# Second MLP's weight conversion in another order, its tiles in other homes, and the reciprocal kept in PSUM

## The chip, the core and the metric

The kernel runs on one core of a Trainium2 chip. Its engines work side by side, each through its own instructions in order: TensorE (PE, matrix products), VectorE (DVE), ScalarE (ACT), GpSimd (POOL); SyncE (SP) issues most of the transfers. The metric is the device time of one execution in microseconds (us), lower is better. Three runs of the kernel before took 1035.93 to 1036.97 us, median 1036.37.

## What is computed

Attention over 4 batches, 8 heads, 576 positions and 64 elements gives x with 2304 rows (tokens) of 512. Two MLPs follow, each with an inner width of 2048; the second one's middle is a rational function:

```python
def _moe_ref(x, w_in, w_out):                  # first MLP
    h = x @ w_in
    g = np.maximum(h, 0.0) + np.log1p(np.exp(-np.abs(h)))
    return g @ w_out

def _moe2_ref(x, w_in, w_out, a, b):           # second MLP
    h = x @ w_in
    P = a[0] + a[1] * h + a[2] * h * h + a[3] * h * h * h
    Q = 1.0 + np.abs(b[0]) * np.abs(h) + np.abs(b[1]) * h * h
    return (P / (Q + 1e-06)) @ w_out
```

Inputs come as float64. A product of nearly full precision is made of three products of rounded parts: each operand is a high part plus a low part (`hi`, `lo`), and hi·hi, hi·lo and lo·hi are summed.

## The kernel before

**Units.** An MLP is worked through in units (phase, T, ff): phase 0 or 1 is the first or second MLP, T a tile of 256 to 512 tokens, ff one of 16 slices of 128 of the inner width. `stage_a` makes h of the unit in a PSUM bank, `stage1` to `stage3` make the middle function and its two parts, `stage_b` adds the unit's share of the second product, three units after `stage_a`. Phase 0 has T 0 to 5; attention is interleaved until T 4 begins. Phase 1, T 0 follows unit by unit (16 units of 384 tokens). T 1 to 3 of phase 1 run in another way: `group` makes four blocks of 256x512 by seven sums of products (`slot`), where combinations of weights (areas `s1` to `s4`) and of tokens take the place of an eighth product; there are four groups to a T. T 4 (`TAIL`) is again 16 units of 384 tokens.

**The second MLP's weights.** 32 blocks (ff, half), half 0 of the first product and half 1 of the second, are loaded raw (512 KB each) and converted while phase 0, T 4 and 5 run (`conv2_to`, one to a unit). `conv_t` (L909 and L911 on DVE, L910 on ACT) makes a float32 tile of tag `tc`; `conv_hl` splits it into hi (ACT L915) and lo (POOL L916). Of each pair of half-0 blocks `sum_make` forms the combinations (DVE, L980 to L983, four instructions), and `sum_split` splits and stores these in the DRAM areas `wa_d` (ACT L991, POOL L992, one store, twice to a pair). The order in the list `c2`: half 1 of ff 0 to 11, both halves of ff 12 to 15, then half 0 of ff 0 to 11.

**Homes.** Half 1 of ff 0 to 11 lies in SBUF areas that attention has left (tags J, Q, V). Half 0 of ff 0 to 11 lies in tag W, where the first MLP's `w1h` of the same number must have been used for the last time. Both halves of ff 12 to 15 are spilled to DRAM (`w2_d`, 16 stores) and reloaded during phase 1, T 0 (`reload2`, 16 loads), half 1 into W. `keep_a` stores half 0 of all 16 into `wa_d` (32 stores), from which T 1 to 4 load 100 tiles `wa` of 512 KB into W, 11 slots ahead (`load_wa`; 7 of them by the end of T 0).

**The quotient.** In phase 1, 1/Q is made as exp(-ln Q) on ACT and corrected on DVE; with `w` = Q, `a` = the reciprocal, `t` = the numerator without its constant:

```python
        nc.scalar.activation(a, w, AF.Ln, bias=qc)                                           # stage2: L1212
        nc.scalar.activation(a, a, AF.Exp, scale=-1.0)                                       # L1213
        nc.vector.scalar_tensor_tensor(w, w, c, a, op0=ALU.add, op1=ALU.mult)                # L1214
        nc.vector.scalar_tensor_tensor(w, w, -2.0, a, op0=ALU.add, op1=ALU.mult)             # L1215
        nc.vector.scalar_tensor_tensor(t, t, nega[:, 0:1], w, op0=ALU.add, op1=ALU.mult)     # L1216
```

Units use this `stage2`, with all operands in SBUF. The groups' blocks use `act2` (L1243 to L1247), which is the same but for the reciprocal, written into h's own bank; the correction L1246 goes to `w` in SBUF. `stage1` reads h last at L1203 (numerator; the groups' L1237).

**Banks.** PSUM has eight banks: four `acc`, two `h`, two `at`. Units of phase 1, T 0 use only the two `h` up to ff 4 and alternate between `h` and `at` from ff 5 on (`hsel`), as do those of T 4. In a group three sums lie in `h` banks (called y, v and w in the code) and one in `at`.

**The order.** Each tile pool hands out buffers in program order. `plan` then simulates the program with a table of costs, orders each engine's instructions by how late each may end, and ties them in that order for all that starts before 936 us of its own time; the rest keeps the program's priorities.

Of the kernel before, what the change touches and what calls it, by code (L numbers as in the profile page):

```python
# [338 lines left out]
def moe_chain_kernel(ctx, tc, qk0, v0, qk, vv, s0, s, w1, w2, ab, out):  # L339
# [658 lines left out]
    def home2(ff, half):  # L998
        if half == 0:
            if ff >= FS:  # L1000
                return t_l("w2h", [128, 512], F32R), t_l("w2l", [128, 512], F32R)
# [9 lines left out]
    def reload2(ff):
        for half in range(2):
            w2_t[ff, half] = home2(ff, half)
            for d, t in zip(w2_d[ff, half], w2_t[ff, half]):
                nc.sync.dma_start(out=f(t), in_=d)
# [190 lines left out]
    def stage2(u):  # L1206
# [466 lines left out]
```

## Time and profile before

| | |
|---|---|
| median of three runs | 1036.37 us |
| the profiled execution | 1037.39 us, its span 1035.6 us |
| PE busy | 1002.6 us (97%) |
| weight loads (beside PE) | 902.5 us (87%) |
| DVE busy | 814.8 us (79%) |
| ACT busy | 803.7 us (78%) |
| POOL busy | 477.5 us (46%) |
| mean granted clock of TensorE | 0.998 |
| moved by DMA | 207.92 MB |

Stages in the span: attention and phase 0 up to T 3 until about 465 us; phase 0, T 4 and 5, from there to 617; phase 1, T 0, from 617 to 697; the groups of T 1 to 3 from 695 to 957; T 4 to the end. A time in the rows counts from the start of the span. An idle time in brackets is that before the instruction, and behind the arrow stands what ended it.

### The profile page before, as it was taken

What the parts mean: (1) busy time and instruction counts of PE and PEld (TensorE: products, weight loads), DVE (VectorE), ACT (ScalarE), POOL (GpSimd) and SP (SyncE); (2) the same over time, 40 slices, a digit from 0 to 9 for tenths busy, and PEclk for the clock granted to TensorE, in tenths of its full rate; (3) what the DMA queues carried; (4) which work ended last, traced back from release to release, by engine and by line L of the source; (5) the groups of instructions that cost most, each with busy time, mean ns of one, the idle gap of its engine ahead of it and who ended that gap; (6) DMA issues with size and microseconds to landing.
All of it is one profiled execution on the core that took longest, in us unless ns stands there. A gap on an engine that the chain in (4) does not pass through costs nothing.

```text
span 1035.6 us, 18274 instructions
## 1 busy us (share of the span) xinstructions
PE 1002.6 (97%) x5924; PEld 902.5 (87%) x5924; DVE 814.8 (79%) x1783; ACT 803.7 (78%) x1652; POOL 477.5 (46%) x464
## 2 busy tenths in 40 slices
PE   6999999999999999999999999998999999999998
PEld 5889999889998888898999888788888898889897
DVE  5788986887987788785455879898789888778865
ACT  5898878877987777777677676788878888787775
POOL 2757664412221121222226766776566457455543
PEclk9999999999999999999999999999999999999999
DMA  9777565665564644436679988969555655654300
GB/s 265 279 241 262 184 223 187 207 187 151 160 199 126 201 147 146 134 118 215 228 241 310 371 282 294 362 210 312 178 164 186 216 187 173 205 169 156 123 1 31
DMA packets 103502, 207.92 MB, mean 201 GB/s; under 512 B 11632, under 2 KB 28848, under 8 KB 103408
## 3 DMA queue, kind: packets, MB, share of 16 engines
q1 hardware_dynamic: 100864, 202.60, 59.3%
q10 hardware_dynamic: 2544, 4.16, 1.6%
q8 instruction: 47, 0.77, 0.3%
q14 instruction: 47, 0.39, 0.1%
HBM read 163.25 MB, written 39.39 MB: 196 GB/s over the span
## 4 chain that ended last, share of the span: by engine, by line
PE 62%; DVE 15%; ACT 9%; issue 5%; POOL 4%; DMA 4%; SPq 0%; DVEq 0%; POOLq 0%; ACTq 0%
PE at L764 5%; PE h L1089 5%; PE h L1090 5%; PE h L1091 5%; PE acc L1127 4%; PE acc L1125 4%; PE acc L1126 4%; PE at L1330 4%; PE h L1330 3%; PE acc L1270 3%; PE at L623 2%; PE acc L1269 2%; PE acc L1268 2%; PE at L624 2%; DVE tc L911 2%
## 5 line engine op out<-in xcount | busy, mean ns | idle before, releaser
L616 POOL TENSOR_SCALAR PA<-PA,stat 128x384 f32<-128x384 f32 (+3 forms) x112 | 72.1, 650 | 172.4 <-DVE stat L615 72.4
L1089 PE MATMUL h<-xs,w1h 128*128 128x448 f32 (+1 forms) x360 | 122.9, 342 | 1.9 <-DVE e L1191 1.9
L1090 PE MATMUL h<-xs,w1h 128*128 128x448 f32 (+1 forms) x360 | 122.5, 340 | 0.0
L1091 PE MATMUL h<-xs,w1l 128*128 128x448 f32 (+1 forms) x360 | 122.2, 340 | 0.0
L1126 PE MATMUL acc<-gl,w1h 128*128 128x448 f32 (+1 forms) x352 | 118.7, 339 | 1.2 <-POOL gl L1387 1.2
L1127 PE MATMUL acc<-gh,w1l 128*128 128x448 f32 (+1 forms) x352 | 119.0, 341 | 0.1
L1125 PE MATMUL acc<-gh,w1h 128*128 128x448 f32 (+1 forms) x352 | 118.6, 340 | 0.0
L1254 POOL TENSOR_TENSOR gl<-PA,gh 128x512 fp32r<-128x512 f32 x48 | 63.7, 1328 | 71.9 <-issue 54.9
L613 ACT ACTIVATE PA<-PA,stat 128x384 f32<-128x384 f32 (+3 forms) x112 | 64.0, 572 | 16.7 <-DVE stat L596 15.6
L1089 PEld LDWEIGHTS h<-xs,w1h 128*128 128x128 f32 x360 | 67.9, 189 | 6.5 <-DVE e L1191 3.1
L1090 PEld LDWEIGHTS h<-xs,w1h 128*128 128x128 f32 x360 | 67.8, 188 | 3.8 <-DVE xs L1054 0.4
L1091 PEld LDWEIGHTS h<-xs,w1l 128*128 128x128 f32 x360 | 67.8, 188 | 3.1
L1126 PEld LDWEIGHTS acc<-gl,w1h 128*128 128x128 f32 x352 | 66.1, 189 | 4.5 <-POOL gl L1387 1.4
L1127 PEld LDWEIGHTS acc<-gh,w1l 128*128 128x128 f32 x352 | 66.0, 188 | 3.8 <-DMA w1l<-l_d 0.3
L1125 PEld LDWEIGHTS acc<-gh,w1h 128*128 128x128 f32 x352 | 66.1, 189 | 3.0 <-ACT gh L1385 0.2
L1187 ACT ACTIVATE e<-h 128x448 f32<-128x448 f32 (+1 forms) x90 | 43.4, 482 | 30.6 <-PE h L1091 28.8
L1387 POOL TENSOR_TENSOR gl<-e,gh 128x256 fp32r<-128x256 f32 (+1 forms) x48 | 47.6, 992 | 33.8 <-ACT gh L1385 28.9
L1268 PE MATMUL acc<-w2b,gh 128*128 128x512 f32 x144 | 57.0, 396 | 0.5 <-ACT gh L1253 0.5
L1269 PE MATMUL acc<-w2b,gh 128*128 128x512 f32 x144 | 56.7, 394 | 0.0
L1270 PE MATMUL acc<-w2b,gl 128*128 128x512 f32 x144 | 55.1, 396 | 0.6 <-POOL gl L1254 0.6
L596 DVE CUSTOM_DVE_ANT_0 PA<-at,mask 128x384 f32<-128x384 f32 (+3 forms) x100 | 50.4, 518 | 5.8 <-PE at L624 4.2
L623 PE MATMUL at<-ht 128*128 128x512 f32 (+3 forms) x156 | 53.3, 347 | 0.6 <-DVE stat L604 0.3
(357 smaller groups left out, 3283.2 us busy)
## 6 DMA issues: line engine op xcount, KB each, us to landing
wa<-wa_d SPq DMA_DIRECT2D x100, 512.0 KB
w1l<-l_d SPq DMA_DIRECT2D x138, 256.0 KB
raw<-in_w_dram SPq DMA_DIRECT2D x48, 512.0 KB
raw<-in_qk_dram SPq DMA_DIRECT2D x24, 384.0 KB
l_d<-w1l SPq DMA_DIRECT2D x32, 256.0 KB
raw64x<-in_w_dram SPq DMA_DIRECT2D x16, 512.0 KB
wa_d<-pt SPq DMA_DIRECT2D x16, 512.0 KB
wa_d<-w2a SPq DMA_DIRECT2D x24, 256.0 KB
```

What stands on the lines that cost most here:

```text
L616: nc.gpsimd.tensor_scalar(pt[:, 0:n], pt[:, 0:n], stat[:, i, 2:3], 1.0, op0=ALU.mult, op1=ALU.mult)
L623: nc.tensor.matmul(o, hq, p.ht[:, 1, k0:k0 + n], start=True, stop=False)
L1089: nc.tensor.matmul(h, wh[:, cs], xh, start=(k == 0), stop=False)
L1090: nc.tensor.matmul(h, wh[:, cs], xl, start=False, stop=False)
L1091: nc.tensor.matmul(h, wl[:, cs], xh, start=False, stop=(k == KD - 1))
L1125: nc.tensor.matmul(o, wh[:, cs], gh, start=first and not both, stop=False)
L1126: nc.tensor.matmul(o, wh[:, cs], gl, start=False, stop=False)
L1127: nc.tensor.matmul(o, wl[:, cs], gh, start=False, stop=last and (not both or m % 2 == 1))
L1268: nc.tensor.matmul(acc[m], gh[:, cs], wh, start=first, stop=False)
L1269: nc.tensor.matmul(acc[m], gh[:, cs], wl, start=False, stop=False)
L1270: nc.tensor.matmul(acc[m], gl[:, cs], wh, start=False, stop=last)
L1330: nc.tensor.matmul(o[:, p * 256:p * 256 + 256], x, z[:, k], start=first and p == k == n == 0, stop=(k, n) == (1, 2), skip_group_check=True)
```

## The change

It does four things. Half-0 blocks are converted first, all 16 of them, then half 1; the 16 half-0 conversions are spread over 19 units, and the half-1 conversions follow, one to a unit, from the fifth unit of T 5 to the fourth of phase 1. Half 0 of ff 0 to 11 takes the homes that attention left, and half 1 of all 16 takes W. Only half 0 of ff 12 to 15 is spilled, straight into its place in `wa_d`, so that 8 stores to and 8 loads from there remain of 16 and 16, and 24 of the 32 stores at T 0. The tiles `wa` go through J, Q and V instead of W (12 places, as before) and are asked for from ff 6 on, 10 of them by the end of T 0. And `quotient` serves both kinds of units: in units from ff 5 on, in T 4 and in the groups the reciprocal and its corrected value both stay in h's bank.

```diff
 def conv2_hl(ff, half, t):
-        if ff >= FS:
+        spill = half == 0 and ff >= FS
+        if spill:
             hi, lo = (tmp_tile("PA", 3, (128, 512), F32R) for _ in range(2))
...
-        if ff >= FS:
-            for d, t in zip(w2_d[ff, half], (hi, lo)):
-                nc.sync.dma_start(out=d, in_=f(t))
+        if spill:
+            store_a(ff, (hi, lo))
...
     def home2(ff, half):
-        if half == 0:
-            if ff >= FS:
-                return t_l("w2h", [128, 512], F32R), t_l("w2l", [128, 512], F32R)
-            t = t_w("w2a", [128, 1024], F32R)
+        if half:
+            t = t_w("w2b", [128, 1024], F32R)
...
         else:
-            t = (t_q if ff < 10 else t_v if ff < FS else t_w)("w2b", [128, 1024], F32R)
+            t = (t_q if ff < 10 else t_v)("w2a", [128, 1024], F32R)
...
     def stage2(u):
...
-        nc.scalar.activation(a, w, AF.Ln, bias=qc)
-        nc.scalar.activation(a, a, AF.Exp, scale=-1.0)
-        nc.vector.scalar_tensor_tensor(w, w, c, a, op0=ALU.add, op1=ALU.mult)
-        nc.vector.scalar_tensor_tensor(w, w, -2.0, a, op0=ALU.add, op1=ALU.mult)
-        nc.vector.scalar_tensor_tensor(t, t, nega[:, 0:1], w, op0=ALU.add, op1=ALU.mult)
+        r, o = (h_t[u],) * 2 if T or ff >= H_ONLY else (a, w)
+        quotient(a, t, w, r, o)
...
+    def quotient(a, t, w, r, o):
+        nc.scalar.activation(a, w, AF.Ln, bias=qc)
+        nc.scalar.activation(r, a, AF.Exp, scale=-1.0)
+        nc.vector.scalar_tensor_tensor(w, w, QC, r, op0=ALU.add, op1=ALU.mult)
+        nc.vector.scalar_tensor_tensor(o, w, -2.0, r, op0=ALU.add, op1=ALU.mult)
+        nc.vector.scalar_tensor_tensor(t, t, nega[:, 0:1], o, op0=ALU.add, op1=ALU.mult)
...
     def act2(bl):
...
+        quotient(a, t, w, bl.h, bl.h)
...
-            t = t_w("wa", [128, 2, 2, 256], F32R)
+            t = home_a()
...
-        c2 = [(ff, 1) for ff in range(FS)] + [(ff, half) for ff in range(FS, NF) for half in range(2)] + [(ff, 0) for ff in range(FS)]
+        c2 = [(ff, half) for half in range(2) for ff in range(NF)]
...
-                if 0 < t4 <= 20:
-                    conv2_to(t4)
-                elif t4 > 20:
-                    conv2_to(min(t4, 32))
+                if t4 > 0:
+                    conv2_to(min(t4 * 16 // 19, 16) if t4 < 20 else min(t4 - 3, 32))
...
-                    keep_a(ff)
+                    if ff < FS:
+                        store_a(ff, w2_t[ff, 0])
...
-                    if ff >= 9:
-                        load_wa(min(ff - 8, 7))
+                    if ff >= 6:
+                        load_wa(min(ff - 5, 10))
```

Until about 450 us every engine's instructions stand as before. Three places after that, all on DVE. The first is phase 0, T 4, between the ends of two units' middle function (`at<-at,e`); `gl` is a unit's lo part, L909 and L911 convert. Before:

```order
L1191 SCALAR_TENSOR_TENSOR at<-at,e 128x448
L1387 TENSOR_TENSOR gl<-at,gh 128x448
L909 TENSOR_SCALAR tc<-raw64x 128x512
L911 SCALAR_TENSOR_TENSOR tc<-raw64x,tc 128x512
L1191 SCALAR_TENSOR_TENSOR h<-h,e 128x448
L1387 TENSOR_TENSOR gl<-h,gh 128x448
L909 TENSOR_SCALAR tc<-raw_7045 128x512
L911 SCALAR_TENSOR_TENSOR tc<-raw_7045,tc 128x512
```

Behind it, the same two units after the change, in whose numbering L907 and L909 convert and L978 to L981 form the sums:

```order
L1194 SCALAR_TENSOR_TENSOR at<-at,e 128x448
L1397 TENSOR_TENSOR gl<-at,gh 128x448
L907 TENSOR_SCALAR tc<-raw64x 128x512
L909 SCALAR_TENSOR_TENSOR tc<-raw64x,tc 128x512
L978 TENSOR_TENSOR tc<-tc 128x256
L979 TENSOR_TENSOR tc<-tc 128x256
L1194 SCALAR_TENSOR_TENSOR h<-h,e 128x448
L980 TENSOR_TENSOR tc<-tc 128x256
L1397 TENSOR_TENSOR gl<-h,gh 128x448
L981 TENSOR_TENSOR tc<-tc 128x256
L907 TENSOR_SCALAR tc<-raw_6849 128x512
L909 SCALAR_TENSOR_TENSOR tc<-raw_6849,tc 128x512
```

Four sums have come between; they stood in T 5 and at the start of phase 1. The second place is phase 1, T 0, from the numerator of its third unit (first row) to that of its fourth (last row). Before:

```order
L1203 SCALAR_TENSOR_TENSOR PA<-PA,prm,h 128x384
L911 SCALAR_TENSOR_TENSOR tc<-raw_7902,tc 128x512
L1163 COPY yb<-at 128x448
L1163 COPY yb<-acc 128x448
L909 TENSOR_SCALAR tc<-raw64x 128x512
L1214 SCALAR_TENSOR_TENSOR tmp<-tmp,e 128x384
L911 SCALAR_TENSOR_TENSOR tc<-raw64x,tc 128x512
L1215 SCALAR_TENSOR_TENSOR tmp<-tmp,e 128x384
L1216 SCALAR_TENSOR_TENSOR PA<-PA,prm,tmp 128x384
L1202 TENSOR_TENSOR PA<-PA,h 128x384
```

After, where L1221 to L1223 are the corrections and L1206 the numerator:

```order
L1206 SCALAR_TENSOR_TENSOR PA<-PA,prm,h 128x384
L1166 COPY yb<-at 128x448
L1221 SCALAR_TENSOR_TENSOR tc<-tc,e 128x384
L907 TENSOR_SCALAR tc<-raw_8026 128x512
L1222 SCALAR_TENSOR_TENSOR tc<-tc,e 128x384
L1221 SCALAR_TENSOR_TENSOR tmp<-tmp,e 128x384
L1223 SCALAR_TENSOR_TENSOR PA<-PA,prm,tc 128x384
L909 SCALAR_TENSOR_TENSOR tc<-raw_8026,tc 128x512
L1222 SCALAR_TENSOR_TENSOR tmp<-tmp,e 128x384
L1205 TENSOR_TENSOR PA<-PA,h 128x384
L1223 SCALAR_TENSOR_TENSOR PA<-PA,prm,tmp 128x384
L1206 SCALAR_TENSOR_TENSOR PA<-PA,prm,h 128x384
```

One conversion and one copy have left this stretch, and corrections of the unit ahead have come in. The third place is a group of T 2, where `h<-at,pt` puts a block into the `h` bank that the block just before it leaves (L1356 before, L1366 after). Before:

```order
L1245 SCALAR_TENSOR_TENSOR P_10092<-P_10092,h 128x512
L1246 SCALAR_TENSOR_TENSOR P_10092<-P_10092,h 128x512
L1356 TENSOR_TENSOR h<-at,pt 128x512
L1247 SCALAR_TENSOR_TENSOR PA<-PA,prm,P_10092 128x512
L1356 TENSOR_TENSOR h<-h,pt 128x512
```

After:

```order
L1221 SCALAR_TENSOR_TENSOR P_10036<-P_10036,h 128x512
L1222 SCALAR_TENSOR_TENSOR h<-P_10036,h 128x512
L1223 SCALAR_TENSOR_TENSOR PA<-PA,prm,h 128x512
L1366 TENSOR_TENSOR h<-at,pt 128x512
L1366 TENSOR_TENSOR h<-h,pt 128x512
```

The last correction now reads the bank and so stands ahead of the instruction that takes the bank over.

## Rows read from the trace of the kernel before

**Rows 1.** Windows by stage: length, busy us of PE, PEld, DVE, ACT, POOL; clock, DMA.

```profile
475.00:580.00 105.00, 105.00 (x518) 96.95 (x518) 61.12 (x92) 74.82 (x139) 42.48 (x33) 1.00 0.79 263
580.00:621.40 41.40, 39.60 (x195) 35.94 (x194) 31.13 (x38) 28.07 (x53) 27.66 (x21) 1.00 0.91 319
621.40:697.00 75.60, 71.22 (x348) 62.30 (x347) 67.03 (x96) 56.48 (x109) 53.01 (x42) 0.98 0.85 295
697.00:722.00 25.00, 22.40 (x147) 19.69 (x146) 21.79 (x29) 20.43 (x37) 17.17 (x14) 1.00 0.85 295
722.00:957.00 235.00, 233.27 (x1441) 207.69 (x1441) 193.37 (x272) 190.31 (x321) 136.48 (x103) 1.00 0.55 183
957.00:1035.60 78.60, 72.90 (x353) 63.32 (x351) 55.17 (x93) 55.25 (x104) 35.52 (x33) 1.00 0.16 51
```

**Rows 2.** Waits of PE, 590 to 725 us: us in total, times, longest.

```profile
PE acc L1132 <- ACT gh L1385: 2.3, 3, 1.4
PE h L1089 <- DVE PA L1203: 2.2, 1, 2.2
PE h L1089 <- DVE e L1191: 1.8, 2, 1.4
PE h L1330 <- issue: 1.2, 1, 1.2
```

**Rows 3.** Waits of PE, 957 to 1035 us.

```profile
PE acc L1132 <- DVE yb L1274: 1.4, 1, 1.4
```

**Rows 4.** Timeline of PE, phase 1, T 0: start, us, instruction, idle before.

```profile
645.83 0.44 PE L1089 MATMUL h<-yt,w2a 128*128 128x384 f32 x1 [2.23 <-DVE PA L1203]
```

**Rows 5.** A window just behind it; the clock stands behind the busy times.

```profile
646.30:649.70 3.40, 3.40 (x12) 3.05 (x11) 3.26 (x6) 2.72 (x6) 1.43 (x2) 0.50 1.03 319
```

**Rows 6.** Timeline of DVE in the same place.

```profile
638.72 1.40 DVE L1214 SCALAR_TENSOR_TENSOR tmp<-tmp,e 128x384 f32<-128x384 f32 x1 [0.49 <-ACT e L1213]
640.04 1.78 DVE L911 SCALAR_TENSOR_TENSOR tc<-raw64x,tc 128x512 int32<-128x512 int32 x1
643.14 1.51 DVE L1216 SCALAR_TENSOR_TENSOR PA<-PA,prm,tmp 128x384 f32<-128x384 f32 x1
```

**Rows 7.** Groups of DVE, 621.4 to 697 us: shapes, count, busy us, mean ns, idle.

```profile
L1203 DVE SCALAR_TENSOR_TENSOR PA<-PA,prm,h 128x384 f32<-128x384 f32 x10 | 6.1, 607 | 0.1
L1214 DVE SCALAR_TENSOR_TENSOR P<-P,e 128x384 f32<-128x384 f32 x4 | 4.4, 1094 | 0.7 <-ACT e L1213 0.7
L1216 DVE SCALAR_TENSOR_TENSOR PA<-PA,prm,P 128x384 f32<-128x384 f32 x4 | 2.4, 610 | 0.0
L911 DVE SCALAR_TENSOR_TENSOR tc<-raw64x,tc 128x512 int32<-128x512 int32 x2 | 3.4, 1686 | 0.1
L909 DVE TENSOR_SCALAR tc<-raw64x 128x512 int32<-128x512 int32 x2 | 1.6, 820 | 0.1
L983 DVE TENSOR_TENSOR tc<-tc 128x256 f32<-128x256 f32 x3 | 2.0, 652 | 0.1
```

**Rows 8.** Groups of DVE, 580 to 621.4 us.

```profile
L911 DVE SCALAR_TENSOR_TENSOR tc<-raw,tc 128x512 int32<-128x512 int32 x3 | 3.6, 1195 | 1.0 <-ACT raw L910 0.9
L980 DVE TENSOR_TENSOR tc<-tc 128x256 f32<-128x256 f32 x3 | 2.9, 977 | 0.3
```

**Rows 9.** Groups of DVE over the span, blocks of T 1 to 3.

```profile
L1246 DVE SCALAR_TENSOR_TENSOR tc<-tc,h 128x512 f32<-128x512 f32 x12 | 8.2, 686 | 0.4
L1247 DVE SCALAR_TENSOR_TENSOR PA<-PA,prm,tc 128x512 f32<-128x512 f32 x24 | 21.8, 909 | 0.4
```

**Rows 10.** Timeline where an `h` bank passes from one block to the next, twice.

```profile
720.02 0.69 DVE L1246 SCALAR_TENSOR_TENSOR tc<-tc,h 128x512 f32<-128x512 f32 x1
720.81 0.59 PE L1330 MATMUL h<-xl,wa 128*128 128x256 f32 x3 [1.17 <-issue]
...
806.85 0.69 DVE L1246 SCALAR_TENSOR_TENSOR tc<-tc,h 128x512 f32<-128x512 f32 x1
807.64 0.36 PE L1330 MATMUL h<-xl,wa 128*128 128x256 f32 x1
```

More of the change, by code (lines that the diff above doesn't have):

```diff
@@ L346, in moe_chain_kernel @@
     l_d = [[dr.tile([128, 512], F32, name=f"l_d{t}_{i}") for i in range(2)] for t in range(NF)]
-    w2_d = {(ff, half): [dr.tile([128, 512], F32, name=f"w2_d{ff}_{half}_{i}") for i in range(2)]
-            for ff in range(FS, NF) for half in range(2)}
     wa_d = [[dr.tile([128, 2, 1024], F32, name=f"wa_d{q}_{d}") for d in range(4)] for q in range(4)]
@@ L1007, in home2, with row_a, store_a @@
         else:
-            t = (t_q if ff < 10 else t_v if ff < FS else t_w)("w2b", [128, 1024], F32R)
+            t = (t_q if ff < 10 else t_v)("w2a", [128, 1024], F32R)
         return t[:, 0:512], t[:, 512:1024]
+    def row_a(ff):
+        q, p, i = ff // 4, ff // 2 % 2, ff % 2
+        return wa_d[q][i][:, p].rearrange("p (b h c) -> p b h c", b=2, h=2)
+    def store_a(ff, ts):
+        for h, t in enumerate(ts):
+            nc.sync.dma_start(out=row_a(ff)[:, :, h], in_=f(t).rearrange("p (b c) -> p b c", b=2))
     def reload2(ff):
[L1012 to L1015, printed above, removed]
+        w2_t[ff, 0] = t_l("w2h", [128, 512], F32R), t_l("w2l", [128, 512], F32R)
+        for h, t in enumerate(w2_t[ff, 0]):
+            nc.sync.dma_start(out=f(t).rearrange("p (b c) -> p b c", b=2), in_=row_a(ff)[:, :, h])
     def segments(T):
@@ L1210, in stage2 @@
         a, t, w = e_t[u]
-        c = QC
+        r, o = (h_t[u],) * 2 if T or ff >= H_ONLY else (a, w)
+        quotient(a, t, w, r, o)
+        e_t[u] = t
+    def quotient(a, t, w, r, o):
         nc.scalar.activation(a, w, AF.Ln, bias=qc)
-        nc.scalar.activation(a, a, AF.Exp, scale=-1.0)
-        nc.vector.scalar_tensor_tensor(w, w, c, a, op0=ALU.add, op1=ALU.mult)
-        nc.vector.scalar_tensor_tensor(w, w, -2.0, a, op0=ALU.add, op1=ALU.mult)
-        nc.vector.scalar_tensor_tensor(t, t, nega[:, 0:1], w, op0=ALU.add, op1=ALU.mult)
-        e_t[u] = t
+        nc.scalar.activation(r, a, AF.Exp, scale=-1.0)
+        nc.vector.scalar_tensor_tensor(w, w, QC, r, op0=ALU.add, op1=ALU.mult)
+        nc.vector.scalar_tensor_tensor(o, w, -2.0, r, op0=ALU.add, op1=ALU.mult)
+        nc.vector.scalar_tensor_tensor(t, t, nega[:, 0:1], o, op0=ALU.add, op1=ALU.mult)
     class Block:
@@ L1306, in moe_chain_kernel, with home_a @@
     wa_t, wa_n, used = {}, [0], [0]
+    wa_free = []
+    def home_a():
+        if not wa_free:
+            wa_free.extend([t_j] * 2 + [t_q] * 6 + [t_v] * 2)
+        al = wa_free.pop(0)
+        if al is not t_j:
+            return al("wa", [128, 2, 2, 256], F32R)
+        if "j" not in keep:
+            t = t_j("wa", [128, 2, 1024], F32R).rearrange("p n (b h c) -> p n b h c", b=2, h=2)
+            keep["j"] = t[:, 1]
+            wa_free.insert(0, t_j)
+            return t[:, 0]
+        return keep.pop("j")
     def load_wa(n):
@@ L1315, in load_wa @@
             wa_n[0] += 1
-    def keep_a(ff):
-        q, p, i = ff // 4, ff // 2 % 2, ff % 2
-        dst = wa_d[q][i][:, p].rearrange("p (b h c) -> p b h c", b=2, h=2)
-        for h, t in enumerate(w2_t[ff, 0]):
-            nc.sync.dma_start(out=dst[:, :, h], in_=f(t).rearrange("p (b c) -> p b c", b=2))
     def slot(T, q, a, b, o, first):
```

5 lines of the change are left out of this document (removed).

## The prediction, made before the changed kernel had run

> **What bounds the kernel now.** I read the windows by stage first [rows 1]. From 475 to 580 us PE has no idle time: its own work is the bound, and whatever DVE or the transfers do there is hidden. The idle time of PE that this change can reach is in four of the other windows: 41.40 - 39.60 = 1.8 us up to 621, 75.60 - 71.22 = 4.4 in the next (phase 1, T 0), 2.6 from 697 to 722, 1.7 in the 235 us of the groups. The last window has 5.7, of which one wait of 1.4 can move [rows 3]; most of the rest lies behind the last product. In the window of T 0, DVE is busy for 67.03 of 75.60 us (89%) and from 697 on for 87%: there it is DVE that PE waits for. The list of waits says the same [rows 2]: 2.2 us for a bank that L1203 on DVE still read, 1.8 for L1191 on DVE, 2.3 for a gh whose quotient DVE had just ended.
>
> The largest single wait is that of 2.23 us at 645.83 [rows 4]. Just ahead of it DVE worked on corrections and a conversion that took 1.40, 1.78 and 1.51 us [rows 6], though the same kinds of instruction take 0.61 elsewhere in the window (L1216 with `P` [rows 7]). POOL is busy for 53 of the 75.6 us [rows 1]; instructions of DVE whose tensors all lie in SBUF are drawn out there, and L1203, which reads h from PSUM, is not: 0.607 us over ten [rows 7]. Behind that wait the granted clock was 0.50 for 3.4 us [rows 5], the lower of the two levels, 1.2 GHz. What 12 products did in this time they would have done in half of it, so the wait of 2.23 us cost a further 1.7. Waits of 1.2 to 1.4 us [rows 2] left the clock of their windows at 1.00 [rows 1].
>
> **The change, part by part.** PE's instructions stay the same; so each part is worth what it does to these waits. Gains are negative.
>
> Sums move from T 5 and phase 1 into T 4 (475 to 580 us). The order puts four sums to two units there. By the slow rows of windows in which conversions and sums already run side by side, two units in T 4 would need on DVE: two middle functions and two lo parts that read PSUM, 4 x 0.61 as L1203 [rows 7], 2.4; two conversions of 0.82 (L909 [rows 7]) and 1.20 (L911 [rows 8]), 4.0; four sums of 0.98 (L980 [rows 8]), 3.9; together 10.3 us. PE did 518 products in 105 us there [rows 1], 0.203 each, 24 to a unit, so 9.8 for two units. With the sums at 0.65 (L983 [rows 7]) DVE's part is 9.0 us. In a window that has this mixture now PE lost 1.8 us (580 to 621 [rows 1]). Bounds: 0 and 0.5 us for each of 8 pairs, 4.0. With DVE at 61 of 105 us now [rows 1], I take **+0.8**.
>
> The store and load of half 1 of four slices goes, 24 transfers of 256 KB on SP's queue in all with the stores of `keep_a`; 8 MB of stores from the sums move into T 4, where the transfers' share is 0.79, from where it is 0.91 [rows 1]. As PE lost little at 0.91 and nothing that names a transfer [rows 2], this is 0 on both sides. Tiles `wa` are asked for earlier; PE did not wait for one [rows 2], 0.
>
> From 580 to 621 the sums thin out on DVE and their splits on POOL. The wait before the first unit of phase 1 (1.4 us, the longest of the two for L1191) stood behind such work. Half-1 conversions still stand there. Between 0 and -1.8 I take **-0.8**.
>
> Phase 1, T 0 (621 to 697). By the order, nine sums leave this stretch, 9 x 0.7 = 6.3 us between L983 and L980 [rows 7, 8], and three conversions come in, 3 x (1.4 + 0.6) = 6.0, L911 being 1.69 at most and L909 0.82 [rows 7]. Exchange for nothing, then. The quotient is what lightens it: of 16 units 11 (ff 5 to 15) keep the reciprocal and its correction in the bank, and the corrections of 9 of these lie in the stretch, 27 instructions. The 42 on L1214 to L1216 took 35.5 us, 0.85 each, between rows of 0.61 and 1.09; with one operand in PSUM I take L1203's 0.607 at most, 0.58 for the three: 27 x 0.27 = 7.3 us. DVE comes down from 67 to 60, below the 69.5 that PE needs (71.22 less the 1.7 of the slow clock). The gain is bounded by what PE lost there, 4.4 + 1.7 = 6.1. It won't all go: the first five units keep their corrections in SBUF, and they are where the long wait is. Between the numerators of units 3 and 4, DVE now has eight instructions ahead, as before: these took 9.1 us, the three longest in [rows 6], with two copies, two L911 and one L909 among them; after, six corrections at 0.85, one conversion and one copy, about 7.7. So the wait of 2.23 becomes 0.8, too short for the slow clock as far as these rows go: -1.4 - 1.7; half of the later waits, -0.9. **-4.0.**
>
> From 697 to 722 the wait of 1.4 us for gh ends behind two corrections of over 1.1 us. They go to 0.58: between 0 and -1.4, with the wait of the next paragraph 0.2 longer, **-1.0**.
>
> The groups (722 to 957). The correction L1247 takes 909 ns from SBUF [rows 9] and would take 690, as L1246 with its PSUM operand does; but PE lost only 1.7 us here, so at most that is gained. Against it: h's bank is now held through the last correction, 0.69 us longer, and the instruction that takes the bank over stands behind it on DVE, as the order shows. This bank is tight. PE's first product into it came 0.10 us after L1246 had ended, both at 720.81 and at 807.64 [rows 10]; the former wait, named "issue", ended with that release. Over eleven groups this gap is 0.1 to 1.5 us, 0.63 in the mean. Two blocks follow each other in that bank to a group, so up to 1.38 us are added to a turn. Less drawn-out work on DVE, about 1 us to a group, should give most of it back: between -1.7 and +8.3, I take **+0.7**.
>
> Here a rule speaks against the change. The rows show no price for an operand in PSUM: 0.607 on L1203 and 0.610 on L1216 from SBUF alone [rows 7]. The Trainium skill ("Perfetto Trace Analysis", Optimizing Scalar/DVE Operations) states an overhead of some 60 ns for an instruction of DVE on SBUF and 125 on PSUM. By that an estimate holds the bank 0.13 us longer to a block, 22 blocks, +2.9 on the sum. I go by the rows.
>
> The last units: the wait of 1.4 for a copy queued on DVE [rows 3] halves, **-0.5**.
>
> Sum: 0.8 - 0.8 - 4.0 - 1.0 + 0.7 - 0.5 = -4.8. The profiled execution took 1037.39 us, so 1032.6; it lies 1.0 above the median of the runs, so the prediction is **1031.6**.
>
> **Rivals.** *The bank becomes the bound (slower).* The turn from block to block in one `h` bank grows by 1.38 us to a group, 0.63 is free, and nothing is given back: 11 x 0.75 = 8.3 instead of 0.7. Sum +2.8, 1039.2. For it: the 0.10 us of [rows 10]. Against it: the planner knows the banks and may hurry those blocks, and DVE, at 193 of 235 us, has room. It decides from 0.5 us lost to a group on. *Given back elsewhere (no change).* T 4 costs its 4.0, as DVE there reaches the slow durations, or the early units of phase 1 stay as they are because conversions replaced the sums one for one: -1.5 for T 0 instead of -4.0, and 1.6 for T 4. Sum -1.6 or -1.5, 1034.9. For it: the even exchange above. *All the waits go.* 1.8 + 6.1 + 2.6 + 1.4 = 11.9, nothing given back: 1024.5. For it: DVE falls below PE in every window.
>
> **How the numbers follow.** 0.50 for the forecast, with 1028 to 1034.5 as its own range, 0.17 for all the waits, 0.17 for no change, 0.16 for the bank. 0.2%, about what a measurement here can tell, is 2.1 us: faster ends at 1034.3. Faster is 0.48 + 0.17 = 0.65, same 0.17 and 0.02 of the forecast's edge, 0.19, slower 0.16. The range leaves out the top half of the bank's case and the bottom of the third: 1024.5 to 1038.5.
>
> **What would show it.** Right: in T 0 the drawn-out corrections (over 1 us) only up to ff 4, those of the later units near 0.58; DVE near 60 us between 621 and 697; no clock of 0.50 there; PE idle under 2.5 us in that window. T 4 right: PE idle under 1 us from 475 to 580. Bank: PE's waits in the groups that end at the last correction, 0.3 us or less to a group. Wrong: a wait of over 2 us in the first five units with the slow clock behind it; idle of PE in T 4; or waits for `h` in each group.

## The result, and the profile after

The changed kernel took 1025.16 us (median of four runs, 1024.60 to 1025.54), the kernel before 1036.15 (four runs): a ratio of 0.9892, 95% interval 0.9875 to 0.9909. The forecast was -4.8 us, the measured change is -11.0. The measured time lies in the predicted range and outside the forecast's own 1028 to 1034.5, next to the rival in which all the waits go (1024.5). The profiled execution took 1024.89 us.

The head of the changed kernel's page:

```profile
span 1023.1 us, 18253 instructions
PE 998.2 (98%) x5924; PEld 903.1 (88%) x5924; DVE 791.1 (77%) x1783; ACT 803.2 (79%) x1652; POOL 466.4 (46%) x464
```

Its windows by stage, cut where the same work begins and ends as in [rows 1], with the same columns (length, busy us of PE, PEld, DVE, ACT, POOL, clock, DMA share, GB/s):

```profile
475.00:580.30 105.30, 105.30 (x520) 97.21 (x519) 70.91 (x107) 74.20 (x140) 48.72 (x37) 1.00 0.95 328
580.30:619.50 39.20, 39.20 (x196) 36.34 (x195) 22.35 (x34) 30.19 (x57) 25.18 (x20) 1.00 0.93 326
619.50:689.20 69.70, 68.79 (x349) 61.65 (x348) 59.92 (x94) 58.08 (x113) 49.05 (x42) 1.00 0.56 184
689.20:712.40 23.20, 21.91 (x148) 20.02 (x148) 18.41 (x26) 18.76 (x34) 13.38 (x12) 1.00 0.72 241
712.40:946.00 233.60, 232.77 (x1436) 207.82 (x1435) 185.49 (x271) 190.36 (x318) 133.43 (x103) 1.00 0.57 186
946.00:1023.10 77.10, 72.83 (x353) 63.46 (x351) 50.26 (x91) 54.61 (x103) 32.61 (x32) 1.00 0.16 52
```

PE's idle time per stage, length less busy, was 0, 1.8, 4.4, 2.6, 1.7 and 5.7 us before and is 0, 0, 0.9, 1.3, 0.8 and 4.3. The second stage has none left. T 4 has 0.95 of the transfers' time and ten more us of DVE, and PE still never waits there. No window has a clock under 1.00.

PE's waits of the changed kernel, 588 to 715 us and, behind the dots, 946 us to the end (total us, times, longest), against [rows 2, 3]:

```profile
PE at L1340 <- ACT pt L1361: 1.3, 1, 1.3
PE acc L1135 <- ACT gh L1395: 0.4, 1, 0.4
PE acc L1137 <- POOL gl L1397: 0.4, 1, 0.4
...
PE acc L1135 <- ACT yb L1274: 0.4, 1, 0.4
```

The waits of 2.2 for h's bank and of 1.8 for the first MLP's middle are gone, that for gh fell from 2.3 in three waits to 0.4 in one, that at the end from 1.4 to 0.4. The one of 1.3 is new; it lies in the groups and ends with ACT's `pt`.

Groups of DVE in the changed kernel between 619.5 and 689.2 us, against [rows 7] (L1221 to L1223 are the corrections that were L1214 to L1216, L909 is the conversion that was L911):

```profile
L909 DVE SCALAR_TENSOR_TENSOR tc<-raw64x,tc 128x512 int32<-128x512 int32 x3 | 3.6, 1201 | 1.5 <-ACT raw64x L908 1.5
L1223 DVE SCALAR_TENSOR_TENSOR PA<-PA,prm,at 128x384 f32<-128x384 f32 x5 | 3.1, 612 | 0.1
L1222 DVE SCALAR_TENSOR_TENSOR at<-tc,at 128x384 f32<-128x384 f32 x5 | 2.8, 560 | 0.1
L1222 DVE SCALAR_TENSOR_TENSOR P<-P,e 128x384 f32<-128x384 f32 x2 | 2.8, 1390 | 0.0
L1221 DVE SCALAR_TENSOR_TENSOR tc<-tc,at 128x384 f32<-128x384 f32 x5 | 2.8, 551 | 2.3 <-POOL gl L1397 1.2 <-ACT at L1220 1.0
L1221 DVE SCALAR_TENSOR_TENSOR P<-P,e 128x384 f32<-128x384 f32 x2 | 2.2, 1099 | 0.0
```

The corrections with an operand in PSUM take 0.55 to 0.61 us; those with all tensors in SBUF, of the first five units, up to 1.39 in the mean of a group. The Trainium skill ("SBUF — State Buffer", Who interferes with whom) states that an instruction of DVE with two SBUF inputs contends with one of GpSimd that reads SBUF, and that one with at most one SBUF input, outside the two-port modes, does not; the pairs P,e and tc,at above agree.

**Where the time went.** I compare when the same work begins in the two profiled executions: the first product of a unit or of a slot (one of the groups' sums). The table has the start after less the start before, in us, here and for the experiments below, which are named in its head by what they do. T 4 begins between 1.5 us early and 1.0 late in kernels with the same plan for the start, so the steps down a column tell more than its totals. (PE's order in the changed kernel differs from before from 411 us on, not only from about 450.)

| first product of | before at | changed | order only | quotient only, 4 rounds | in groups only, 4 rounds | old order, bank all | DVE early | DVE late |
|---|---|---|---|---|---|---|---|---|
| phase 0, T 4 | 447.3 | 0.3 | -0.4 | 1.0 | -0.6 | -0.7 | -1.5 | -1.3 |
| phase 1, T 0 | 617.6 | -1.8 | -2.4 | 0.8 | -0.9 | -1.8 | -3.6 | -3.3 |
| the first slot | 694.8 | -7.7 | -8.8 | 4.2 | -1.0 | -1.8 | -4.3 | -7.2 |
| the eighth slot | 713.8 | -9.7 | -5.2 | 2.1 | -1.1 | -3.9 | -6.2 | -4.5 |
| the last slot | 949.3 | -11.0 | -5.0 | 0.2 | -1.8 | -6.1 | -7.6 | -5.5 |
| (the last product) | 1031.4 | -12.5 | -4.6 | -1.4 | -3.7 | -7.2 | -9.5 | -6.9 |

The changed kernel gains 2.1 us up to phase 1, 5.9 in its T 0, 2.0 in the first seven slots, 1.3 in the rest of the groups, 1.4 in the last units. The profiled executions differ by 12.5 us and the medians by 11.0, since that of before lay 1.2 above its median.

### The profile page after: what moved, and what is told of

The parts are those of the page before. It is cut to its first block, busy times and chain, and to the rows that moved or that the text cites. A ratio compares the mean times of both kernels' runs of the same rounds, so it can differ in the third digit from the quotient of the medians.

```text
span 1023.1 us, 18253 instructions
## 1 busy us (share of the span) xinstructions
PE 998.2 (98%) x5924; PEld 903.1 (88%) x5924; DVE 791.1 (77%) x1783; ACT 803.2 (79%) x1652; POOL 466.4 (46%) x464
## 5 line engine op out<-in xcount | busy, mean ns | idle before, releaser
L1269 PE MATMUL acc<-w2b,gh 128*128 128x512 f32 x192 | 75.9, 395 | 0.0
L1270 PE MATMUL acc<-w2b,gh 128*128 128x512 f32 x192 | 75.8, 395 | 0.0
L1271 PE MATMUL acc<-w2b,gl 128*128 128x512 f32 x192 | 73.7, 395 | 0.0
```

The lines of the kernel that those rows point to most:

```text
L1269: nc.tensor.matmul(acc[m], gh[:, cs], wh, start=first, stop=False)
L1270: nc.tensor.matmul(acc[m], gh[:, cs], wl, start=False, stop=False)
L1271: nc.tensor.matmul(acc[m], gl[:, cs], wh, start=False, stop=last)
```

## The experiments

**The halves.** The change has an order (conversions, sums, homes) and a quotient. Two kernels have one each. The order only is the changed kernel with the old places of the reciprocal and its correction:

```diff
-        r, o = (h_t[u],) * 2 if T or ff >= H_ONLY else (a, w)
+        r, o = a, w
...
-        quotient(a, t, w, bl.h, bl.h)
+        quotient(a, t, w, bl.h, w)
```

The quotient only is the kernel before with the changed `quotient` in `stage2` and `act2`:

```diff
+        r, o = (h_t[u],) * 2 if T or ff >= H_ONLY else (a, w)
+        quotient(a, t, w, r, o)
...
+        quotient(a, t, w, bl.h, bl.h)
```

Of the order only:

> The changed kernel with the quotient as before (units: everything in SBUF; groups: reciprocal in the bank, correction in SBUF). What stays is the order of the conversions, the homes and the earlier wa. If the order is the main part, it holds 7 of the 11 us: 1029. If the quotient is the main part (DVE's corrections kept from being drawn out), the order alone gives the 2 us at the end of phase 0, T 5 and little of phase 1, T 0: 1033. If both must come together to get DVE below PE in T 0, this one and the next add up to clearly less than 11.

Measured: 1031.39 us, ratio 0.9961 [0.9946, 0.9975].

Of the quotient only:

> The kernel before with the quotient alone changed. Quotient as main part: 6 to 7 us faster, 1029 to 1030, of which 1.5 in the last units, 1 to 3 in the groups and their start, the rest in T 0 from ff 5 on; the first units of T 0 still show the wait of about 2 us with the clock of 0.50 behind it. Order as main part: 3 us, 1033.

Measured: 1036.1 us, ratio 1.0001 [0.9992, 1.001]. So -4.6 and 0 alone, and -11.0 together: neither half carries the gain, and 6.4 us come only from both; 4.7 of them are left when the start of the program is held the same (below).

The two other cuts take the quotient back from the changed kernel in one place each. The groups' correction goes back to SBUF (`bl.h, bl.h` to `bl.h, w`):

> The changed kernel, the groups' corrected reciprocal back in SBUF, so the bank is released one instruction earlier and the last correction reads SBUF only. If holding the bank costs anything in the groups (my forecast: +0.7 net), this is equal or up to 1 us faster than the changed kernel, 1024 to 1025. If the quicker last correction (909 to about 690 ns) is worth more than the bank, it is 1 to 3 us slower, 1026 to 1028, with the time lost between the first and the last group.

Measured: 1026.96 us, ratio 0.9911 [0.9896, 0.9926]. And the units' quotient goes back to SBUF (`r, o = a, w`):

> The changed kernel, the quotient of the units (T 0 from ff 5 on, and T 4) back in SBUF, the groups as changed. By the forecast the quotient brings most of the gain in the second half of T 0, 27 instructions shorter by 0.27 us: 3 us slower there, 1 us slower in T 4 and 1 at the start of the groups, so 1029 to 1030. If the order of the conversions did it, less than 1 us slower than the changed kernel, 1026.

Measured: 1031.15 us, ratio 0.9953 [0.9939, 0.9966]. Behind the new order the quotient is worth 1.8 us in the groups and 6.0 in the units.

Order only gains 6.4 us in T 0 and gives 3.7 of them back in the first seven slots. Its windows: T 0 from its first product to the first slot, the next seven slots, and, behind the dots, the stretch with the slow clock.

```profile
615.20:686.00 70.80, 68.23 (x345) 61.59 (x343) 64.53 (x87) 54.52 (x107) 47.33 (x38) 1.00 0.58 180
686.00:708.70 22.70, 21.15 (x121) 18.25 (x122) 21.14 (x28) 16.66 (x31) 16.11 (x12) 0.92 0.47 149
...
688.70:692.10 3.40, 3.40 (x13) 2.92 (x12) 3.40 (x5) 2.66 (x6) 2.29 (x3) 0.50 0.00 1
```

The kernel before and the changed kernel, cut at the same places:

```profile
617.60:694.80 77.20, 72.81 (x350) 63.94 (x351) 68.64 (x97) 57.82 (x111) 52.65 (x43) 0.98 0.86 294
694.80:713.80 19.00, 17.57 (x115) 15.48 (x114) 15.91 (x23) 14.83 (x28) 15.78 (x13) 1.00 0.75 259
```

```profile
615.80:687.10 71.30, 70.39 (x354) 63.25 (x353) 60.52 (x95) 59.04 (x115) 48.39 (x42) 1.00 0.57 189
687.10:704.10 17.00, 17.00 (x115) 15.64 (x114) 14.34 (x21) 12.34 (x23) 11.93 (x10) 1.00 0.48 146
```

With the order alone DVE comes to the end of T 0 late: it is busy for 21.14 of the next 22.70 us, where PE idles for 1.6 and has the slow clock for 3.4. In the changed kernel DVE has 4.0 us less to do in T 0 and 6.8 less in the next seven slots, and PE idles not at all there.

**The start of the program.** The kernel with the quotient only began its unit 48 2.8 us later than before, long before any edited line runs. The planner makes six plans and takes the one that it reckons shortest. In the kernel before, the changed one and the order alone that is the fourth; with the quotient in the old order it is the sixth, which also puts the first 176 us of PE's work into another order. I first took the quotient out of the units of T 0 (`if T` instead of `if T or ff >= H_ONLY`):

> The order of before with the new quotient only in the groups and in the last units, not in phase 1, T 0. With the quotient in T 0 too the old order came out at 1036.1 us: T 0 then lost 7.2 us more than before at its unit 106 (a wait of 4.28 us and 6.8 us at a granted clock of 0.50), and gave them back in the groups and at the end. Theory A (the quotient gains in the groups whatever the order is, and its loss in T 0 hides it): T 0 as before, with one wait near 2.2 us, and some 4 us gained between the first slot and the end, 1031 to 1033 us. Theory B (in the groups it gains only behind the new order): 1035 to 1036.5 us.

Measured: 1036.62 us, ratio 1.0004 [0.9995, 1.0013]. It looks like theory B, but this kernel has the sixth plan too and began unit 48 4.6 us late. With `ROUNDS` at 4 instead of 6 the fourth plan is taken and the start reads as before. The quotient everywhere, then in the groups and last units only:

> The order of before with the new quotient everywhere, as in the earlier run of the quotient alone (1036.1 us), but the planner is held to four rounds. With six, it took its sixth plan, which also stood PE's first 176 us in another order, and unit 48 began 2.8 us later than before; of four it takes the fourth, as in the kernel before, and the start reads row for row as before. Theory A (the quotient gains some 4 us where it stands, and the start hid that): unit 48 within 0.7 us of before, and 1031.5 to 1034 us in all. Theory B (without the new order phase 1, T 0 eats the gain, with waits of over 2 us and the slow clock behind them): 1035 to 1037.5.

> The order of before with the new quotient in the groups and the last units alone, the planner held to four rounds. In the earlier run (1036.6 us) unit 48 began 4.6 us later than before and the end came 0.4 us later, so 4.2 us were gained behind the start. Theory A (that gain is the quotient's, whatever the start): unit 48 within 0.7 us of before, 1031.5 to 1033.5 us. Theory B (the groups only caught up what they had lost, since another resource bounds them): 1035 to 1036.5.

Measured: 1034.42 us, ratio 0.9981 [0.9972, 0.999], and 1033.78 us, ratio 0.9974 [0.9964, 0.9985]; the first lies between its theories, the second 0.3 above theory A. Unit 48 came 1.2 late and 0.4 early. So in the old order the quotient is worth 2.4 us in the groups and the last units, about as in the new one (1.8 in the groups, and some 0.6 in the last units by the profiled executions). In the units of T 0 it brings nothing (0.6 us slower, with intervals that overlap), where behind the new order the units of T 0 and T 4 gain 6.0 together. That is where the two halves need each other: -4.6 for the order, some -2 for the groups, the rest for the units.

With the quotient everywhere (four rounds) T 0 takes 80.6 us. Its window, and the one with the slow clock:

```profile
618.40:699.00 80.60, 73.32 (x353) 65.25 (x354) 67.47 (x102) 59.93 (x117) 51.75 (x45) 0.96 0.82 287
...
659.20:666.00 6.80, 5.01 (x12) 3.95 (x13) 5.11 (x10) 6.74 (x15) 4.42 (x5) 0.50 1.06 368
```

The wait of PE in the same place, from its timeline:

```profile
660.99 0.79 PE L1132 MATMUL acc<-w,gh 128*128 128x512 f32 x1 [4.26 <-ACT gh L1383]
```

That gh waits for a unit among the first five, whose corrections stay in SBUF, behind four sums and beside the sums' splits on POOL. To see whether it is these corrections, one more kernel (four rounds, old order) keeps the quotient in the bank in all units (`r, o = (h_t[u],) * 2`):

> The order of before (planner held to four rounds) with the new quotient in the groups and in all units of phase 1, T 0, the first five included, whose corrections stay in SBUF in the run at 1034.4 us. Theory A (in the old order the quotient's gain is lost at one place, where the first units' corrections in SBUF run beside the sums' splits on POOL, with a wait of 4.3 us and 6.8 us at a granted clock of 0.50): that wait and the slow clock go or fall under 2 us, 1028 to 1031.5. Theory B (the old order loses it whatever the corrections take there: the sums, their splits and the conversions themselves hold PE up, or two banks are too few): 1032.5 to 1036.

Measured: 1031.79 us, ratio 0.9957 [0.9943, 0.997], between the two theories. The wait for gh went, and one of 3.9 us for h's bank came, with 3.4 us at a clock of 0.50 behind it. Its window of T 0:

```profile
615.80:693.10 77.30, 71.95 (x354) 65.41 (x355) 60.73 (x102) 60.31 (x117) 51.99 (x46) 0.98 0.89 305
```

The wait, from PE's timeline:

```profile
641.52 0.44 PE L1089 MATMUL h<-yt,w2a 128*128 128x384 f32 x1 [3.88 <-DVE PA L1220]
```

The timeline of DVE in the units ahead of it (L1218 and L1219 are corrections here, L909 and L911 the conversion, L980 and L981 sums):

```profile
623.53 1.21 DVE L909 TENSOR_SCALAR tc<-raw64x 128x512 int32<-128x512 int32 x1
624.85 1.60 DVE L911 SCALAR_TENSOR_TENSOR tc<-raw64x,tc 128x512 int32<-128x512 int32 x1
626.55 1.33 DVE L980 TENSOR_TENSOR tc<-tc 128x256 f32<-128x256 f32 x1
627.81 0.54 DVE L1218 SCALAR_TENSOR_TENSOR P<-P,h 128x384 f32<-128x384 f32 x1
628.27 1.04 DVE L981 TENSOR_TENSOR tc<-tc 128x256 f32<-128x256 f32 x1
```

DVE's work in T 0 is 60.73 us, as in the changed kernel, and T 0 still takes 77.3 us instead of 71.3. In the old order it is not the amount alone. A conversion and a sum, 4.1 us, stand ahead of this unit's first correction, and three more sums between and behind its corrections.

The bank that PE waits for at 641.52 is held by the next unit, ff 1, and this unit waits for a buffer. Tag `tc` has three: converted blocks, their sums and the Q of every second unit share them, and a pair's buffers come free as POOL splits it. The unit's first step on ACT (the amount of h, into an `e` buffer), the splits, and the start of its Q:

```profile
625.02 0.47 ACT L1198 ACTIVATE e<-h 128x384 f32<-128x384 f32 x1
632.41 3.27 POOL L992 TENSOR_TENSOR pt<-tc,pt 128x512 fp32r<-128x512 f32 x2
635.71 0.71 ACT L1199 ACTIVATE tc<-e,prm 128x384 f32<-128x384 f32 x1
```

Its Q begins 10.7 us after its first step, as the second split ends. In the kernel before it is 13.0 us, again at the end of a split, and ff 1 then holds one of the two `e` buffers, so that ff 3 begins on ACT (643.23) only behind a correction of ff 2. On ff 3's numerator hangs the wait of 2.23 us at 645.83 [rows 4]:

```profile
626.78 0.47 ACT L1198 ACTIVATE e<-h 128x384 f32<-128x384 f32 x1
638.40 1.30 POOL L992 TENSOR_TENSOR pt<-tc,pt 128x512 fp32r<-128x512 f32 x1 [0.65 <-DVE tc L909]
639.74 0.71 ACT L1199 ACTIVATE tc<-e,prm 128x384 f32<-128x384 f32 x1
643.23 0.49 ACT L1198 ACTIVATE e<-h 128x384 f32<-128x384 f32 x1 [0.74 <-DVE tmp L1215]
```

In the changed kernel, without sums in T 0, it is 5.0 us, with the order alone 1.3:

```profile
624.12 0.49 ACT L1201 ACTIVATE e<-h 128x384 f32<-128x384 f32 x1
629.12 0.69 ACT L1202 ACTIVATE tc<-e,prm 128x384 f32<-128x384 f32 x1
```

In the six profiled kernels of the old order it is 10.7 to 13.0 us, each time up to the end of a split; in the fourteen of the new order it is 0.9 to 5.0. That the sums hold the units up by these buffers is read from the traces; neither the sums nor the number of buffers was changed alone, so how much of T 0 it makes is not shown.

**DVE's amount in the new order.** Small products that nothing uses were added to the changed kernel, 128x128 in SBUF, four to a unit in nine units of T 0, on DVE or on POOL:

> The changed kernel with 36 more products of 128x128 on DVE, in SBUF, four to a unit in nine units of phase 1, T 0 (they compute nothing that is used). At an estimated 0.15 to 0.25 us each, from 0.61 us for 128x384, these are 5 to 9 us, so DVE's work in T 0 comes back to the 67 to 69 us that it had before. Theory A (the amount of work on DVE sets PE's waits there, as the prediction had it): 3 to 6 us slower, 1028 to 1031. Theory B (it is not the amount but which instructions stand in a row: the sums with their splits): under 1.5 us, 1025 to 1026.7.

> The changed kernel with 36 more products of 128x128 on POOL, in SBUF, at the same places as in the run with them on DVE. At an estimated 0.3 to 0.45 us each, from 1.1 us for 128x384, POOL's work in T 0 rises by 11 to 16 us, from 48 of 71 us to about 62. Theory A (work of POOL is what costs in T 0, through gl and drawn-out instructions of DVE): 3 us or more, 1028 or more, and corrections with all tensors in SBUF take longer than the 1.1 to 1.4 us of the changed kernel. Theory B (POOL has room, its load is not what went): under 1.5 us, 1025 to 1026.7.

Measured: 1028.34 us, ratio 0.9917 [0.9903, 0.9931], and 1025.34 us, ratio 0.9890 [0.9876, 0.9904]. They tell nothing of T 0: as nothing held them there, the planner put all 36 into the first 53 us of the program. The next ones read the unit's numerator, so they must stand ahead of its last correction (four rounds). This is the early one on DVE; the late ones have `ff >= 8`, those on POOL `nc.gpsimd`:

```diff
+        if T == 0 and ff < 8:
+            for _ in range(3):
+                nc.vector.tensor_tensor(keep["zz"], t[:, 0:128], t[:, 0:128], op=ALU.mult)
         quotient(a, t, w, r, o)
```

> The changed kernel with 24 more products of 128x128 on DVE in phase 1, T 0, three to a unit in units 0 to 7, each on the numerator of its unit, so that it stands between the numerator and the first correction (the earlier attempt, with nothing to hold them, was put at the very start of the program by the planner, and cost 3.2 us there). At the 0.29 us that one took then, 7.0 us more on DVE in the first half of T 0. Theory A (the amount of work on DVE sets PE's waits there): 2 to 6 us slower than the changed kernel, 1027 to 1031, with waits of over 1.4 us in that half. Theory B (what went is the rows of sums, not an amount): 1024.5 to 1026.5.

> The same 24 products on DVE in units 8 to 15 of phase 1, T 0: 7.0 us more in its second half, where the changed kernel has 28 us of work in 36, and the one with the old quotient in the units had 2 us more and lost some 4 us between the last units and the first seven products of the groups. Theory A (what DVE has not done at the end of T 0 is paid when the groups begin): 3 to 6 us slower, 1028 to 1031, the loss after unit 106 and before the seventh product. Theory B (DVE has room there, 8 us of it): 1024.5 to 1026.5.

Measured: 1029.18 us, ratio 0.9932 [0.9918, 0.9945], and 1030.91 us, ratio 0.9952 [0.9938, 0.9967]. Against 1024.86, the median of all eight runs of the changed kernel, that is +4.3 and +6.1: theory A in both halves. The products were dearer than expected, 14.1 and 15.5 us in all. They stand inside their unit's own chain, so a longer unit and more work on DVE are not told apart here. The early kernel's waits of PE for gh, 580 to 760 us, where the changed kernel has 0.4:

```profile
PE acc L1135 <- ACT gh L1398: 3.4, 2, 2.3
```

The added products of the late one (shortest, median and longest ns, first and last start):

```profile
L1217 DVE TENSOR_TENSOR zz<-PA x24: 278/662/1277, 660.4 to 695.3; 128x128 f32<-128x128 f32 x24
```

Its windows of T 0, of the seven slots and of the slow clock:

```profile
614.30:687.60 73.30, 70.67 (x354) 63.29 (x353) 68.04 (x111) 58.06 (x112) 48.51 (x41) 1.00 0.57 184
687.60:709.30 21.70, 19.54 (x115) 17.00 (x114) 18.02 (x28) 13.50 (x26) 14.01 (x11) 0.92 0.47 146
...
703.50:706.90 3.40, 3.40 (x19) 3.40 (x18) 2.57 (x4) 1.97 (x4) 1.83 (x2) 0.50 0.40 91
```

The late kernel loses 2.7 us between the first and the eighth slot, where the order alone lost 3.7, and has the slow clock there too: what DVE has not done by the end of T 0 is paid when the groups begin.

The same on POOL:

> The changed kernel with 24 more products of 128x128 on POOL in units 0 to 7 of phase 1, T 0, three to a unit, each on the numerator of its unit, at the places where the same products on DVE cost 4.0 us. At the 0.40 us that one took on POOL in the earlier run, 9.6 us more work on POOL, which has 23 of 36 us in that half. Theory A (POOL's load is a cause of its own: it draws out DVE's instructions in SBUF and delays gl): 2 us slower or more, 1027 to 1031. Theory B (the cause is DVE's amount, POOL has room): 1024.5 to 1026.3.

> The same 24 products on POOL in units 8 to 15 of phase 1, T 0, at the places where they cost 5.8 us on DVE: 9.6 us more on POOL, which has 25 of 36 us there. Theory A (POOL's load is a cause of its own): 2 us slower or more, 1027 to 1031. Theory B (DVE's amount alone): 1024.5 to 1026.3.

Measured: 1027.05 us, ratio 0.9908 [0.9894, 0.9923], and 1026.02 us, ratio 0.9900 [0.9886, 0.9915]: +2.2 and +1.2 against 1024.86, for 13.7 and 11.0 us of work. The early one reaches theory A's bound, the late one stays in theory B. By the products' own durations a us more on POOL cost 0.1 to 0.2 us, a us more on DVE 0.3 to 0.4. POOL's load is at most a smaller cause beside DVE's: with the early products DVE's own work in T 0 rose too, to 63.28 us from 60.52, and the runs of the late kernel (1024.59 to 1027.36) overlap those of the changed one (1023.54 to 1025.68).

The transfers, by 24 more stores (`store_a`'s tiles to another place):

> The changed kernel with 24 more stores of 256 KB on SP's queue in phase 1, T 0: the halves of twelve slices that are stored there anyway are stored a second time, to another place. These 6.3 MB are about what the new order took from this stretch (DMA share 0.86 before, 0.57 after). Theory A (transfers are hidden there, as the prediction had it): within 0.7 us of the changed kernel, 1024.5 to 1026. Theory B (part of the order's gain of 4.6 us is the traffic that went): 1027 to 1030.

Measured: 1025.96 us, ratio 0.9897 [0.9884, 0.9911], +1.1 against 1024.86 at a DMA share of 0.81 instead of 0.57 in T 0; theory A, at the edge of its range.

**The bank.** The changed kernel (four rounds) with the quotient in h's bank in the first five units too, where only two banks go round:

> The changed kernel with the reciprocal and its correction in h's bank in the first five units of phase 1, T 0 as well, where only two banks go round (from unit 5 on there are four). Their 15 corrections took 1.1 to 1.4 us in SBUF and would take some 0.56 to 0.61, as those of the later units, so DVE has some 9 us less to do in that half, where PE loses no more than 0.9 us in the changed kernel; each bank is held two corrections longer, some 2 us. Theory A (a bank held to the last correction becomes the bound where it comes round soon): PE waits for h in the first units, 1027 to 1033. Theory B (the banks have room, and DVE's relief is worth up to what PE still loses): 1023.5 to 1025.5.

Measured: 1023.94 us, ratio 0.9884 [0.9868, 0.9901], theory B. It was run again, with the changed kernel beside it:

> The kernel with h's bank held to the last correction in all units, once more, beside the changed kernel on the same chip. If DVE's relief in the first five units is a gain (theory B of its first run), it lies 0.7 to 1.7 us below the changed kernel, 1023.3 to 1024.6; if the two banks are short there, at or above it.

> The changed kernel itself, once more, as the measure for the run beside it: 1024.6 to 1025.7 us, as in its first four runs.

Measured: 1023.49 us, ratio 0.9879 [0.9864, 0.9894], and 1024.21 us, ratio 0.9884 [0.9868, 0.99]. Over both batches the medians are 1023.9 (eight runs) and 1024.9 (eight runs), each kernel's runs spreading over 3.2 and 2.1 us: a lead of about 1 us, too small to call settled. Its windows of T 0 and of the seven slots:

```profile
614.50:684.80 70.30, 69.69 (x354) 63.57 (x353) 57.09 (x96) 59.15 (x115) 46.73 (x41) 1.00 0.60 191
684.80:701.80 17.00, 17.00 (x116) 15.63 (x115) 11.94 (x19) 11.32 (x22) 11.79 (x10) 1.00 0.59 185
```

DVE's work falls by another 3.4 us in T 0, where 9 were expected, and T 0 by 1.0: PE has little left to lose.

## Why the prediction came out too small

The direction, the places and the engine (DVE ahead of PE in phase 1, T 0) were right. Every term was too careful, and one had the wrong sign. The two that missed most are T 0, where the step from DVE's work to PE's waits failed, and the groups, where a bank was taken for tight that PE does not wait for.

| term of the sum | forecast | measured, profiled executions |
|---|---|---|
| sums moved into T 4 | +0.8 | 0.0 |
| 580 to 621 us | -0.8 | -2.1 |
| phase 1, T 0 | -4.0 | -5.9 |
| 697 to 722 us | -1.0 | -2.0 |
| the groups | +0.7 | -1.3 |
| the last units | -0.5 | -1.4 |

*T 4.* The 10.3 us of DVE for two units against 9.8 of PE were reckoned with the slow durations; PE did not wait once, with DVE at 70.9 of 105.3 us. The lower bound, 0, was right.

*580 to 621.* I took 0.8 of 1.8; all of PE's idle time there went. The order alone gives the same 2.0.

*Phase 1, T 0.* The step on DVE's amount held: 67 to 60 was forecast for the window of [rows 1], 59.9 was measured, the corrections at 0.55 to 0.61 where 0.58 was taken, the drawn-out ones only in the first five units. What failed is the step from DVE's work to PE's waits: the wait of 2.23 us was to become 0.8 and half of the later ones to stay. No wait over 0.4 us is left in T 0. The work between the numerators of units 3 and 4 was to fall from 9.1 to 7.7 us and fell to 5.9: its six corrections took 4.2 us instead of 5.1, its conversion 1.1 instead of 2.0. The two numerators begin 6.2 us apart (632.62, 638.82) instead of 10.5 (634.70, 645.16), and those 4.3 us are more than the wait. With the order alone it is 5.7 us and the wait for h's bank is gone too; with the quotient alone it is 10.5 and the wait stays at 2.2. So the long wait goes with the order, though no correction of these units left SBUF. What the prediction did not see is the chain above, from the sums' buffers to the numerator of ff 3, its unit 4. "Exchange for nothing" was right in amount and wrong in effect. Counted in the traces of before and of the order alone, 11 sums of 7.0 us left T 0 and six instructions of conversions, 6.0 us, came in; the order alone still gains 6.4 us there, of which 2.7 remain after the first slots.

The 1.7 us for the slow clock were too many. Of 73 more runs of the kernel before, 21 have a mean granted clock of 1.000 and a median of 1035.94 us; 35 have 0.998 or less, as one stretch of 3.4 us at 0.50 makes it, and 1036.34. The means differ by 0.5 us (95% interval 0.0 to 0.9).

The quotient also frees the `e` buffer at ACT's exponential instead of DVE's second correction, a second way in which it could gain. Before, ACT waits 10.1 us in T 0 for such a correction before a unit's first step, in the changed kernel 2.4, with the units' quotient in SBUF again 3.5. So behind the new order this explains little of the 6.0.

*697 to 722.* I saw the wait for gh, not that DVE's backlog of the whole T 0 is paid there (DVE late, order only).

*The groups.* The bank is held longer, as forecast, and it costs nothing. DVE's timeline in the changed kernel at one handover, against [rows 10]:

```profile
850.31 0.68 DVE L1222 SCALAR_TENSOR_TENSOR h<-P,h 128x512 f32<-128x512 f32 x1
851.03 0.75 DVE L1223 SCALAR_TENSOR_TENSOR PA<-PA,prm,h 128x512 f32<-128x512 f32 x1
851.88 0.70 DVE L1366 TENSOR_TENSOR h<-at,pt 128x512 f32<-128x512 f32 x1
```

The next block's first instruction on the bank comes 0.89 us after L1222, behind L1223, and PE's idle time in the groups fell from 1.7 to 0.8 of some 234 us. The last correction takes 0.75 us there instead of 0.91 in [rows 9], and with the correction in SBUF again the kernel is 1.8 us slower. The 1.38 us per group were added to a turn that PE does not wait for: the 0.10 us that I took for a tight bank had no idle time of PE ahead of it at 807.64 [rows 10], and where DVE takes the bank, as here, its own queue puts the taker right behind the release. The rival on the bank falls with it, in the new order also where two banks go round (bank in all units); in the old order, with the same two banks, a held bank did cost a wait of 3.9 us. By an estimate from the Trainium skill's overhead for PSUM ("Perfetto Trace Analysis", Optimizing Scalar/DVE Operations) the sum would have been 2.9 higher. The runs show no such price: 0.545 us for a correction wholly in SBUF that POOL leaves alone (L1221 in the changed kernel's T 0), 0.551 with one operand in PSUM.

*The rivals.* "All the waits go" had 11.9 us, 1024.5, at 0.17, and it is what came. Its reason, that DVE falls below PE in every window, does not carry it: DVE's busy time was below PE's in every window of [rows 1] already, 67.03 to 71.22 us in T 0, and at 60.73 in the old order 5.3 us of waits for h stayed. That the sum came within 0.7 us is partly luck: it held 1.7 for the clock and nothing for the groups, which gained 1.3.

## What to carry to other kernels

Comparing an engine's busy time with the bound engine's doesn't tell how much of a wait goes. Follow the longest wait back, step by step, to the instruction or the buffer that each step stood behind. Where the change takes such a link away, cut the whole wait from the sum, not half of it. What the engine hasn't done by the end of one stage is asked back at the next. Ask also which buffers the work shares with the units beside it: taking the same amount out elsewhere doesn't free them. And with a planner in the kernel, see first that the untouched part of the program kept its order, since another plan for the start alone can hide what an edit gains.

## What the runs showed of the hardware

The same wait can be followed by the slow clock or not. Before, PE's wait of 2.23 us was followed by 3.4 us at 0.50, that is 1.2 GHz [rows 4, 5]. The kernel with the quotient in the groups only has the same wait, and its clock stayed at 1.00. From its timeline of PE:

```profile
644.90 0.44 PE L1089 MATMUL h<-yt,w2a 128*128 128x384 f32 x1 [2.23 <-DVE PA L1203]
```

Its window around it:

```profile
640.00:660.00 20.00, 15.84 (x77) 13.02 (x76) 16.65 (x23) 14.91 (x29) 15.43 (x13) 1.00 0.96 317
```

In the order alone it fell at 688.7 us, just behind a wait of 1.24 us:

```profile
687.62 0.50 PE L1135 MATMUL acc<-w2b,gh 128*128 128x512 f32 x1 [1.24 <-ACT gh L1395]
```

One kernel's runs differ in it as well, by their mean clock (21 and 35 of the 73 above). So the prediction's "too short for the slow clock" can't be read from one trace.

Small instructions of DVE are drawn out as well: a product of 128x128 took 0.28 us at best and up to 1.39 in T 0, the same on POOL 0.39 to 0.87.
